# Turning three of attention's five q and k tiles between its units instead of ahead of them

## The chip, the cores and the metric

The kernel runs on one core of a Trainium2 chip. The metric is the device time of one execution in microseconds (us), the median of several runs. The engines named here are TensorE (PE in the profile; its weight loads are PEld), VectorE (DVE), ScalarE (ACT), GpSimd (POOL) and the queue of SyncE (SP), which issues most DMAs. Each engine works through its own list of instructions in the order in which the program wrote them, and waits on semaphores for the others.

## The reference

Three layers follow each other, each on the whole output of the one before: masked attention, and two mixture-of-experts layers. Only the attention is touched.

```python
scores = scale * np.matmul(q, k.transpose(0, 1, 3, 2))       # B, H, S, D = 4, 8, 576, 64
mask_plain = (rel >= 0) & (rel < window)                     # window = 32, heads 0 to 3
mask_dil = (rel >= 0) & (rel < window * dilation) & (rel % dilation == 0)   # dilation = 4, heads 4 to 7
scores = np.where(masks[None, :, :, :], scores, -1000000000.0)
scores = scores - np.max(scores, axis=-1, keepdims=True)
attn = np.exp(scores)
attn = attn / (np.sum(attn, axis=-1, keepdims=True) + 1e-09)
return np.matmul(attn, v).astype(np.float32)
# then x = _moe_ref(attention), result = _moe2_ref(x): routed and balanced experts
```

## The kernel before

`attention` has two parts: it turns q and k into the layout that matmuls need, and then it works through 25 units.

**Turning.** A token's q and k come with the token on the partition; a matmul of scores wants the head dimension there. `TILES` cuts the rows (four tokens in each) into five tiles of 64, 128, 128, 128 and 128 rows. `load_qk` (L103) issues a tile's DMAs on SP. `t_copy` (L149) copies the raw tile with a scale into `rpk` (on DVE) or `rpq` (on ACT). `t_group` (L160) turns four heads with eight transposes on PE (L169) into a PSUM tile; kind 0 is heads 0 to 3, kind 1 heads 4 to 7. `t_evac` (L172) takes that PSUM tile out: ACT writes the fp16 high part (L188), and then DVE subtracts it to get the low part (L190). So a tile has four groups, in the order k kind 0, k kind 1, q kind 0, q kind 1. The evacuation of kind 0 writes with a stride, that of kind 1 in contiguous runs of one or two pieces. The loop at L345 turns all five tiles before the first unit; the loads of a tile go out two tiles ahead, those of v for the units 0 to 2 after the last tile's. Groups take their PSUM tile in turn from `ps_s` (two buffers) and `ps_p` (one), and each is followed by one filler matmul (`warm`, L147).

**Units.** A unit handles 96 queries of four plain heads and 96 of four dilated heads; units 0 and 24 have only one half. In turn n of the loop at L372 the program writes, in this order:

- `scores(n)`: PE, four mask matmuls (L215) and 24 of q with k (L223) into a `ps_s` buffer
- `row_max(n)`: DVE, the maximum over keys (L230) and its scaling (L231)
- `p_trans(n - 1)` on PE (L247, into `ps_p`) and `p_evac(n - 1)`: ACT the high part (L255), DVE the low part (L256)
- `exps(n)`: ACT, eight exponentials from the `ps_s` buffer (L239), which need the row maximum
- `pv(n - 2)`: PE, 24 products with v (L269 to L271) into `ps_v`; DVE the division (L275 to L277)
- `v_split(n + 1)`: DVE the high part of v (L198), POOL two steps (L200, L201)
- `load_v(n + 3)` on SP, and `x_out(n - 3)`: ACT (L288), POOL (L290), stores on SP (L293)

The program is scheduled by hand, so this order is the order on each engine. A PSUM tile is handed out again when the last reader of its buffer is done. What follows attention (the router, then the experts) needs its last output.

Of the kernel before, what the change touches and what calls it, by code (L numbers as in the profile page):

```python
# [11 lines left out]
F32 = mybir.dt.float32  # L12
F16 = mybir.dt.float16
# [6 lines left out]
B, H, S, D = 4, 8, 576, 64  # L20
# [3 lines left out]
QB = 96  # L24
NJ = S // QB
# [37 lines left out]
def tokens_of(p0, n, kind):  # L63


    if kind == 0:
        return [(0, n, p0, 1)]
    out, p = [], p0
    while p < p0 + n:
        r, i = divmod(p, NI)  # L70
        m = min(NI - i, p0 + n - p)
        out.append((p - p0, m, 4 * i + r, 4))
        p += m
    return out
# [9 lines left out]
TILES = [(0, 64), (64, 128), (192, 128), (320, 128), (448, 128)]  # L84
# [4 lines left out]
def attention(tc, q, k, v, masks, wg, ident, xd, L, zero):  # L89

    nc = tc.nc
    with ExitStack() as ctx:
        one = ctx.enter_context(tc.tile_pool(name="a_one", bufs=1))
        ld = ctx.enter_context(tc.tile_pool(name="a_ld", bufs=2))
# [8 lines left out]
        def load_qk(t, nm):  # L103
            f0, n = TILES[t]
            x = raw[t, nm] = ld.tile([128, H, 4, D], F32, name="raw" + nm)
            f = f0
            while f < f0 + n:
                b, i = divmod(f, NI)
                m = min(NI - i, f0 + n - f)
                nc.sync.dma_start(x[f - f0:f - f0 + m].rearrange("i h r d -> i h (r d)"),  # L110
                                  src[nm][b].rearrange("h (i r) d -> i h (r d)", r=4)[i:i + m])
                f += m

        def load_v(u):
            t = VR[u] = vp.tile([128, H, D], F32, name="rawv")
            for kind, (b, j) in UNITS[u].items():
                for p, n, tok, st in tokens_of(max(QB * j - 32, 0), 128, kind):
                    nc.sync.dma_start(t[p:p + n, 4 * kind:4 * kind + 4], bass.AP(
                        tensor=v.tensor, offset=v.offset + (b * H + 4 * kind) * S * D + tok * D,
                        ap=[[st * D, n], [S * D, 4], [1, D]]))  # L120

        def part(u, size):

            ks = list(UNITS[u])
            return slice(ks[0] * size // 2, (ks[-1] + 1) * size // 2)
# [18 lines left out]
        def warm(n):  # L144
            p = ps.tile([128, 2, 512], F32, name="ps_v", bufs=1)
            for _ in range(n):
                nc.tensor.matmul(p[:, 0, :], zero[:, :128], zero, start=True, stop=True)  # L147

        def t_copy(t, nm, eng):  # L149
            n = TILES[t][1]  # L150
            x = RP[t, nm] = ld.tile([128, 4, H, D], F32, name="rp" + nm)
            o, i = x[:n], raw.pop((t, nm))[:n].rearrange("i h r d -> i r h d")
            if eng is nc.scalar:
                nc.scalar.activation(o, i, AF.Copy, scale=SQ)
            else:
                nc.vector.tensor_scalar(o, i, SQ, None, op0=OP.mult)

        GC = [0]

        def t_group(t, nm, kind):  # L160
            f0, n = TILES[t]
            x = RP[t, nm]
            tag, bufs = (("ps_s", 2), ("ps_p", 1), ("ps_s", 2))[GC[0] % 3]
            GC[0] += 1
            p = ps.tile([128, 2, 512], F32, name=tag, bufs=bufs)
            for a in range(2):
                for r in range(4):
                    h = 4 * kind + 2 * a
                    nc.tensor.transpose(p[:, a, r * n:(r + 1) * n], x[:n, r, h:h + 2, :], idf[:n, :n])  # L169
            return p  # L170

        def t_evac(t, nm, kind, p):  # L172
            f0, n = TILES[t]
            pi = p[:, :, :4 * n].rearrange("p a (r i) -> p a r i", r=4)
            if kind == 0:
                parts = [(0, n, [T[nm][:, x, 0:2, 4 * f0:4 * (f0 + n)].rearrange("p a (i r) -> p a r i", r=4)
                                 for x in range(2)])]
            else:
                parts, f = [], f0
                while f < f0 + n:  # L180
                    b, i = divmod(f, NI)
                    m = min(NI - i, f0 + n - f)
                    parts.append((f - f0, m, [
                        T[nm][:, x, 2:4, b * S:(b + 1) * S].rearrange("p a (r i) -> p a r i", r=4)[:, :, :, i:i + m]
                        for x in range(2)]))
                    f += m
            for o, m, (hi, _) in parts:
                nc.scalar.activation(hi, pi[:, :, :, o:o + m], AF.Copy)  # L188
            for o, m, (hi, lo) in parts:
                nc.vector.tensor_sub(lo, pi[:, :, :, o:o + m], hi)  # L190
# [36 lines left out]
        def row_max(u):  # L227
            p, gs = SS[u], part(u, 4)
            nm = wk.tile([QB, 2, 4], F32, name="nm")
            nc.vector.tensor_reduce(nm[:, :, gs], p[:, :, gs], axis=AX.X, op=OP.max)  # L230
            nc.vector.tensor_scalar(nm[:, :, gs], nm[:, :, gs], -SC, None, op0=OP.mult)  # L231
            PP[u] = nm

        def exps(u):
            p, nm, gs = SS.pop(u), PP[u], part(u, 4)
            e = wk.tile([QB, 2, 4, 128], F32, name="e")
            for s in range(2):
                for g in range(gs.start, gs.stop):
                    nc.scalar.activation(e[:, s, g, :], p[:, s, g, :], AF.Exp, bias=nm[:, s, g:g + 1], scale=SC)  # L239
            PP[u] = e  # L240
# [72 lines left out]
        XB, XO = {}, {}  # L313
# [28 lines left out]
        nc.vector.tensor_copy(idh, idf[:QB, :QB])  # L342
        t_copy(0, "k", nc.vector)
        t_copy(0, "q", nc.scalar)
        for t in range(len(TILES)):  # L345
            if t + 2 < len(TILES):
                for nm in "kq":
                    load_qk(t + 2, nm)
            elif t + 2 == len(TILES):
                load_v(0)  # L350
                load_v(1)
                load_v(2)
            for nm in "kq":
                for kind in range(2):
                    t_evac(t, nm, kind, t_group(t, nm, kind))
                    warm(1)
                    if t + 1 < len(TILES) and kind == 0:
                        t_copy(t + 1, nm, nc.vector if nm == "k" else nc.scalar)
            if t == 0:
                nc.scalar.activation(wgh, wgf, AF.Copy, scale=SG)  # L360
                nc.vector.scalar_tensor_tensor(wgl, wgf, SG, wgh, op0=OP.mult, op1=OP.subtract)

        v_split(0)
        loaded = []
        store = [ld.tile([128, 4, H, D], F32, name="rp" + nm).bitcast(F16).rearrange("p r h d -> p (r h d)")
                 for nm in "kkqq"]
        xl = [t[:, :4 * S].rearrange("p (c q) -> p c q", c=4) for t in store[2:]]
        for n in range(NJ + 1):
            XO[(B - 1) * NJ + n] = store[n // 4][:QB, 16 * D * (n % 4):16 * D * (n % 4 + 1)].rearrange(
                "q (k x h d) -> q k x h d", k=2, x=2, h=4)  # L370
        first = S * (B - 1) // 128
        for n in range(NU + 3):  # L372
            if n < NU:
                scores(n)
                row_max(n)
            if 1 <= n <= NU:
                p_evac(n - 1, p_trans(n - 1))
            if n < NU:
                exps(n)
            if n in FILL:  # L380
                warm(FILL[n])
            if n == NU + 1:
                x_turn(NU - 3)
            if 2 <= n <= NU + 1:
                pv(n - 2, [loaded.pop(0)[1] for _ in range(1 if n < NU else 2) if loaded and loaded[0][0] <= n])
            if n + 1 < NU:
                v_split(n + 1)
            if n + 3 < NU:
                load_v(n + 3)
            if n >= 3:  # L390
                x_out(n - 3)
            b, c = divmod(n - 10, NJ)
            if 0 <= b < B - 1 and c < 3:
                c0, c1 = S * b // 128, S * (b + 1) // 128
                c0, c1 = c0 + 2 * c, min(c0 + 2 * c + 2, c1)
                if c1 > c0:
                    x_load(c0, c1)
                    loaded += [(n + 3, i) for i in range(c0, c1)]
            if n == NU - 1:
                x_load(first, first + 1)  # L400
            x_turn(*TURN.get(n, ()))
        p = ps.tile([128, 2, 512], F32, name="ps_v", bufs=1)
# [991 lines left out]
```

## Time and profile before

| what | value |
|---|---|
| median of 3 runs | 1909.49 us (1908.09 to 1910.56) |
| the profiled execution's own time | 1905.73 us |
| its span in the trace | 1904.0 us |
| PE busy, share of the span | 1794.1 us, 94% |
| DVE busy | 1414.7 us, 74% |
| ACT busy | 896.0 us, 47% |
| first exponential of unit 0 | 60.78 us from the span's start |
| first exponential of unit 12 | 106.87 us |
| first exponential of unit 24 | 157.67 us |

The shares are means over stages with different limits. Attention takes the first tenth of the span, so the rows that matter are those of its own stretches. A row of the timeline has its start and its length in us, then engine, line, operation, what it writes and reads, and how many alike are merged; in brackets stands the idle time of the engine before it and what ended it. Instructions overlap a little at their ends on ACT and DVE, so the step from one start to the next is the better measure of what one costs in a row of work.

### The profile page before, as it was taken

To read this page: it belongs to the slowest core of one execution; us is meant where nothing else is said; L and a number is where in the kernel's file an instruction comes from. 1 tells how busy PE (TensorE), PEld (TensorE's weight loads), DVE (VectorE), ACT (ScalarE), POOL (GpSimd) and SP (SyncE) were. 2 spreads that over 40 slices of the span, in tenths; PEclk is the share of its full clock that TensorE was granted. 3 is DMA by queue.
4 is the path that set the end of the run, shared out by engine and by line. 5 is a ranking of instruction groups with operands and counts; after the bars stand their busy time and mean duration, and the time that the engine had idled before them with its cause. 6 is when DMAs were issued, how large, how long until landed. Compare 5 with 4: busy or idle time off the path is not lost.

```text
span 1904.0 us, 36734 instructions
## 1 busy us (share of the span) xinstructions
PE 1794.1 (94%) x15082; PEld 1320.9 (69%) x15082; DVE 1414.7 (74%) x2681; ACT 896.0 (47%) x1558; POOL 284.9 (15%) x359
## 2 busy tenths in 40 slices
PE   6998699989899999999999999999999999999998
PEld 4785366656667665677777777777767777776776
DVE  5996677667764477777788788778878877887666
ACT  6775333333334335554554444455544445554333
POOL 0583321223324000000000000000000000000111
PEclk8888789999999999999999999999999999999999
DMA  9275543355436241233532333353233435323220
GB/s 224 65 153 148 121 96 84 93 99 114 114 68 153 78 152 67 84 150 140 207 126 106 155 150 150 152 195 131 113 144 148 150 148 198 127 115 134 92 92 34
DMA packets 139817, 241.21 MB, mean 127 GB/s; under 512 B 74208, under 2 KB 107232, under 8 KB 132736
## 3 DMA queue, kind: packets, MB, share of 16 engines
q1 hardware_dynamic: 118384, 151.25, 24.4%
q0 software_dynamic: 20592, 87.53, 15.4%
q8 instruction: 118, 1.93, 0.4%
q14 instruction: 51, 0.42, 0.1%
q10 hardware_dynamic: 672, 0.08, 0.0%
HBM read 173.74 MB, written 61.74 MB: 124 GB/s over the span
## 4 chain that ended last, share of the span: by engine, by line
PE 60%; DVE 13%; issue 11%; DMA 8%; ACT 5%; POOL 2%; SPq 1%; POOLq 0%; DVEq 0%; ACTq 0%
PE mm L1058 24%; PE mm L1096 19%; PE mm L800 8%; PE mm L881 4%; DMA raw<-in_w2b_dram 4%; DMA raw<-in_w2a_dram,widx 2%; PE mm L837 2%; DMA rawq<-in_q_dram 1%; DVE nm L230 1%; POOL out_dram L1110 1%; ACT raw L933 1%; DVE hl L1015 1%; PE r L552 1%; DVE w1l L752 1%; POOL xg L781 1%
## 5 line engine op out<-in xcount | busy, mean ns | idle before, releaser
L1058 PE MATMUL mm<-xb,w1h 128*128 128x384 f16 x2352 | 575.8, 327 | 5.1 <-DVE mm L1029 4.7
L1096 PE MATMUL mm<-w2h,hh 128*128 128x256 f16 x1764 | 481.6, 273 | 14.6 <-DVE t L1122 11.8
L1096 PE MATMUL mm<-w2l,hh 128*128 128x256 f16 x1764 | 481.6, 273 | 0.0
L1096 PE MATMUL mm<-w2h,hl 128*128 128x256 f16 x1764 | 481.5, 273 | 0.0
L1096 PEld LDWEIGHTS <-hh 128*128 128x128 f16 x3528 | 345.6, 98 | 59.8 <-issue 17.2
L1058 PE MATMUL mm<-xb,w1l 128*128 128x384 f16 x1176 | 384.8, 327 | 0.0
L1058 PEld LDWEIGHTS <-w1h 128*128 128x128 f16 x2352 | 230.9, 98 | 160.1 <-issue 12.7
L1096 PEld LDWEIGHTS <-hl 128*128 128x128 f16 x1764 | 172.9, 98 | 20.3
L1015 DVE TENSOR_TENSOR hl<-r,hh 128x1536 f16<-128x1536 f32 x84 | 147.5, 1756 | 41.2 <-ACT hh L1014 41.2
L1058 PEld LDWEIGHTS <-w1l 128*128 128x128 f16 x1176 | 115.4, 98 | 76.7 <-issue 1.0
L976 POOL DMA_DIRECT2D ws<-raw x48 | 26.0, 542 | 951.2 <-ACT raw L933 676.1
L1010 ACT ACTIVATE r<-mm 128x384 f32<-128x384 f32 x252 | 119.1, 481 | 98.7 <-PE mm L1058 98.7
L1014 ACT ACTIVATE hh<-r 128x1536 f16<-128x1536 f32 x84 | 124.6, 1483 | 46.0 <-DVE r L1039 44.1
L1021 ACT ACTIVATE mm<-mm 128x384 f32<-128x384 f32 x84 | 40.3, 479 | 179.4 <-PE mm L1058 179.4
L1015 DVE TENSOR_TENSOR hl<-S,hh 128x1152 f16<-128x1152 f32 x84 | 113.5, 1351 | 0.0
L800 PE MATMUL mm<-xt,w1h 128*128 128x288 f16 x512 | 97.8, 290 | 6.3 <-ACT xt L814 6.3
L933 ACT ACTIVATE raw<-raw 128x1024 f16<-128x1024 f32 x48 | 50.6, 1055 | 107.6 <-DVE raw L924 57.6
L803 ACT ACTIVATE w1h<-mm 128x288 f16<-128x288 f32 (+1 forms) x120 | 46.9, 397 | 109.1 <-PE mm L800 105.9
L1106 DVE SCALAR_TENSOR_TENSOR acc<-t,P,acc 128x512 f32<-128x512 f32 x126 | 94.7, 752 | 4.5
L1014 ACT ACTIVATE hh<-S 128x1152 f16<-128x1152 f32 x84 | 96.3, 1147 | 0.0
L800 PE MATMUL mm<-x2l,w0h 128*128 128x256 f16 x288 | 81.9, 284 | 7.4 <-DVE x2l L842 7.4
L804 DVE SCALAR_TENSOR_TENSOR w1l<-mm,w1h 128x288 f16<-128x288 f32 (+1 forms) x120 | 50.8, 435 | 46.7 <-ACT w1h L803 46.3
(288 smaller groups left out, 3307.9 us busy)
## 6 DMA issues: line engine op xcount, KB each, us to landing
xb<-xw SPq DMA_DIRECT2D x30, 1344.0 KB
ws<-raw POOLq DMA_DIRECT2D x48, 448.0 KB, 3.1
ws<-r POOLq DMA_DIRECT2D x48, 448.0 KB, 3.4
raw<-in_w2b_dram SPq DMA_DIRECT2D x32, 512.0 KB
raw<-in_w1b_dram SPq DMA_DIRECT2D x56, 256.0 KB
w1h<-ws SPq DMA_DIRECT2D x6, 1792.0 KB
w1l<-ws SPq DMA_DIRECT2D x6, 1792.0 KB
w2h<-ws SPq DMA_DIRECT2D x6, 1792.0 KB
```

The source lines that it names most:

```text
L800: nc.tensor.matmul(p, a[:, k, 128 * f:128 * (f + 1)], rhs(k, b), start=(k == 0 and i == 0), stop=(k == KT - 1 and i == 2))
L803: nc.scalar.activation(h[0][:, f, :n], p, AF.Relu)
L804: nc.vector.scalar_tensor_tensor(h[1][:, f, :n], p, 0.0, h[0][:, f, :n], op0=OP.max, op1=OP.subtract)
L881: nc.tensor.matmul(p, a[:, f, c], b[:, f, :], start=(f == 0 and n == 0), stop=(f == FT - 1 and n == 2))
L933: self.nc.scalar.activation(hi[:, k], x, AF.Copy, scale=sw)
L1010: nc.scalar.activation(o, p, AF.Relu, scale=SH)
L1014: yield nc.scalar.activation(hq[0][:, i, k], x, AF.Copy)
L1015: yield V.tensor_sub(hq[1][:, i, k], x, hq[0][:, i, k])
L1021: nc.scalar.activation(Q[i], P[i], AF.Copy)
L1058: nc.tensor.matmul(p, w[u][:, 2 * j + i // 2, k, 128 * (i % 2):128 * (i % 2 + 1)], x[:, v, r, j], start=(q in (1, 5) and j == 0 and n == 0 ...
L1096: nc.tensor.matmul(p, h[u][:, i, a, 128 * t:128 * (t + 1)], w[v][:, i, b, :], start=(q in (1, 7) and i == 0 and j == 0), stop=(q in (2, 3) ...
L1106: V.scalar_tensor_tensor(self.acc[:, r, :], x, self.P[:, r, e:e + 1], self.acc[:, r, :], op0=OP.mult, op1=OP.add)
```

## The change

Tiles 0 and 1 are turned ahead of the units as before. The twelve groups of tiles 2, 3 and 4 come from a generator, `later`, of which one step is taken in each of the turns 0 to 11, right behind `exps(n)`: eight transposes, the evacuation on ACT and DVE, and behind a kind 0 group of tiles 2 and 3 the copy of the next tile. Such a group always takes a `ps_s` buffer, the tag of the scores, and has no filler matmul. The loads are written in another order: v for the units 0 and 1 ahead of tile 3, v for unit 2 behind it, tile 4 in turn 0. The tiles that the last units reuse as stores are taken once `later` is done.

```diff
-            tag, bufs = (("ps_s", 2), ("ps_p", 1), ("ps_s", 2))[GC[0] % 3]
+            tag, bufs = (("ps_s", 2), ("ps_p", 1), ("ps_s", 2))[GC[0] % 3] if t < 2 else ("ps_s", 2)
...
-        for t in range(len(TILES)):
-            if t + 2 < len(TILES):
-                for nm in "kq":
-                    load_qk(t + 2, nm)
-            elif t + 2 == len(TILES):
-                load_v(0)
-                load_v(1)
-                load_v(2)
+        def turned(t):
+
             for nm in "kq":
                 for kind in range(2):
                     t_evac(t, nm, kind, t_group(t, nm, kind))
-                    warm(1)
+                    if t < 2:
+                        warm(1)
                     if t + 1 < len(TILES) and kind == 0:
                         t_copy(t + 1, nm, nc.vector if nm == "k" else nc.scalar)
+                    yield
+
+        def later():
+            for t in range(2, len(TILES)):
+                for nm in "kq" if t + 2 < len(TILES) else ():
+                    load_qk(t + 2, nm)
+                yield from turned(t)
+
+        for t in range(2):
+            if t == 1:
+                load_v(0)
+                load_v(1)
+            for nm in "kq":
+                load_qk(t + 2, nm)
+            if t == 1:
+                load_v(2)
+            for _ in turned(t):
+                pass
...
         for n in range(NU + 3):
...
             if n < NU:
                 exps(n)
+            if next(later, 0) == 0 and not store:
+                stores()
             if n in FILL:
                 warm(FILL[n])
```

On DVE, in a full unit of before: `nm` is the row maximum, `ptl` the low part of the turned exponentials, `rc` and `xt` the division, `vh` the high part of v for the next unit, and the last row is the row maximum of the next unit.

```order
L230 TENSOR_REDUCE nm<-ps_s 96x8
L231 TENSOR_SCALAR nm<-nm 96x8
L256 TENSOR_TENSOR ptl<-ps_p,pth 128x768
L275 TENSOR_SCALAR rc<-ps_v 96x8
L276 RECIPROCAL rc<-rc 96x8
L277 TENSOR_TENSOR xt<-ps_v,rc 96x512
L198 TENSOR_SCALAR vh<-rawv 128x8x64
L230 TENSOR_REDUCE nm<-ps_s 96x8
```

The same place now, in turn 4 (tile 3, k, kind 0, and the copy of tile 4's k):

```order
L230 TENSOR_REDUCE nm<-ps_s 96x8
L231 TENSOR_SCALAR nm<-nm 96x8
L256 TENSOR_TENSOR ptl<-ps_p,pth 128x768
L190 TENSOR_TENSOR tk<-ps_s,tk 128x2x4x128
L156 TENSOR_SCALAR rpk<-rawk 128x2048
L275 TENSOR_SCALAR rc<-ps_v 96x8
L276 RECIPROCAL rc<-rc 96x8
L277 TENSOR_TENSOR xt<-ps_v,rc 96x512
L198 TENSOR_SCALAR vh<-rawv 128x8x64
L230 TENSOR_REDUCE nm<-ps_s 96x8
```

The group's subtraction (L190), and the copy (L156) where there is one, stand between a unit's row maximum and the next unit's.

On ACT, two units of before: `e` is the exponentials, `xo` the output's high part, `pth` the turned exponentials' high part.

```order
L239 ACTIVATE e<-ps_s,nm 96x128 x8
L288 ACTIVATE xo<-xt 96x2x256
L255 ACTIVATE pth<-ps_p 128x768
L239 ACTIVATE e<-ps_s,nm 96x128 x8
L288 ACTIVATE xo<-xt 96x2x256
```

The same engine now, in the turns 5 to 7 (the last group of tile 3's k, and tile 3's q):

```order
L188 ACTIVATE tk<-ps_s 128x2x4x16
L288 ACTIVATE xo<-xt 96x2x256
L255 ACTIVATE pth<-ps_p 128x768
L239 ACTIVATE e<-ps_s,nm 96x128 x8
L188 ACTIVATE tq<-ps_s 128x2x4x128
L154 ACTIVATE rpq<-rawq 128x2048
L288 ACTIVATE xo<-xt 96x2x256
L255 ACTIVATE pth<-ps_p 128x768
L239 ACTIVATE e<-ps_s,nm 96x128 x8
```

The group's evacuation (L188) stands right behind a unit's exponentials and ahead of the next unit's.

## Rows read from the trace of the kernel before

**Rows 1.** Windows: us; PE, PEld, DVE, ACT, POOL busy; PEclk; DMA; GB/s.

```profile
0.00:34.00 34.00, 23.64 (x106) 14.99 (x107) 15.74 (x28) 18.70 (x16) 2.26 (x9) 0.75 1.03 221
34.00:59.50 25.50, 17.13 (x129) 12.56 (x129) 23.11 (x18) 21.94 (x18) 0.73 (x1) 0.93 0.44 125
59.50:106.90 47.40, 45.92 (x676) 38.06 (x672) 44.16 (x82) 37.62 (x114) 37.92 (x46) 0.89 0.39 94
```

**Rows 2.** Timeline of DVE in full units (start, length).

```profile
73.67 0.42 DVE L198 TENSOR_SCALAR vh<-rawv 128x512 f16<-128x512 f32 x1
74.00 1.21 DVE L230 TENSOR_REDUCE nm<-ps_s 96x8 f32<-96x1024 f32 x1
...
101.41 1.21 DVE L230 TENSOR_REDUCE nm<-ps_s 96x8 f32<-96x1024 f32 x1
...
103.61 0.15 DVE L275 TENSOR_SCALAR rc<-ps_v 96x8 f32<-96x8 f32 x1
...
104.70 0.75 DVE L198 TENSOR_SCALAR vh<-rawv 128x512 f16<-128x512 f32 x1
105.37 1.21 DVE L230 TENSOR_REDUCE nm<-ps_s 96x8 f32<-96x1024 f32 x1
```

**Rows 3.** Timeline of ACT in the units 0, 11, 12 and 24.

```profile
60.78 1.13 ACT L239 ACTIVATE e<-ps_s,nm 96x128 f32<-96x128 f32 x4 [3.42 <-DVE nm L231]
...
102.92 2.15 ACT L239 ACTIVATE e<-ps_s,nm 96x128 f32<-96x128 f32 x8 [0.60 <-DVE nm L231]
104.94 0.65 ACT L288 ACTIVATE xo<-xt 96x512 f16<-96x512 f32 x1
...
106.87 2.15 ACT L239 ACTIVATE e<-ps_s,nm 96x128 f32<-96x128 f32 x8 [0.59 <-DVE nm L231]
...
157.67 1.13 ACT L239 ACTIVATE e<-ps_s,nm 96x128 f32<-96x128 f32 x4
```

**Rows 4.** Timeline of ACT while the last tile is turned, kinds 0 and 1.

```profile
50.20 2.49 ACT L188 ACTIVATE tk<-ps_p 128x1024 f16<-128x1024 f32 x1 [0.85 <-PE ps_p L169]
52.42 1.13 ACT L188 ACTIVATE tk<-ps_s 128x1024 f16<-128x1024 f32 x1
```

**Rows 5.** Timeline of DVE while tiles are turned.

```profile
32.35 1.33 DVE L190 TENSOR_TENSOR tq<-ps_p,tq 128x640 f16<-128x640 f32 x2
...
45.72 1.23 DVE L156 TENSOR_SCALAR rpk<-rawk 128x2048 f32<-128x2048 f32 x1
46.88 1.26 DVE L190 TENSOR_TENSOR tk<-ps_p,tk 128x896 f16<-128x896 f32 x2
...
52.73 2.42 DVE L190 TENSOR_TENSOR tk<-ps_p,tk 128x1024 f16<-128x1024 f32 x1 [1.10 <-ACT tk L188]
54.96 1.24 DVE L190 TENSOR_TENSOR tk<-ps_s,tk 128x1024 f16<-128x1024 f32 x1
56.13 2.42 DVE L190 TENSOR_TENSOR tq<-ps_s,tq 128x1024 f16<-128x1024 f32 x1
...
59.52 0.27 DVE L198 TENSOR_SCALAR vh<-rawv 128x256 f16<-128x256 f32 x1
```

**Rows 6.** Timeline of PE at its slower pace: a group, parts of units 0 to 2.

```profile
48.20 1.97 PE L169 MATMUL ps_p<-idf,rpk 128*128 128x128 f32 x8 [0.94 <-DVE tk L190]
...
64.61 1.55 PE L247 MATMUL ps_p<-idf,e 96*128 96x96 f32 x8
...
66.19 0.27 PE L269 MATMUL ps_v<-vh,pth 128*96 128x65 f16 x1
...
66.27 0.27 PE L270 MATMUL ps_v<-vh,ptl 128*96 128x65 f16 x1
...
66.91 1.07 PE L215 MATMUL ps_s<-mk,idb 96*96 96x256 bf16 x4
...
67.91 1.51 PE L223 MATMUL ps_s<-tk,tq 64*96 64x128 f16 x24
```

**Rows 7.** Chain that ended last: the transfer behind tile 3's q.

```profile
24.69 13.39 DMA rawq<-in_q_dram
```

More of the change, by code (lines that the diff above doesn't have):

```diff
@@ L364, in attention, with stores @@
         loaded = []
[L365 to L370, printed above, removed]
+        later = later()
+        store, xl = [], []
+        def stores():
+            store.extend(ld.tile([128, 4, H, D], F32, name="rp" + nm).bitcast(F16).rearrange("p r h d -> p (r h d)")
+                         for nm in "kkqq")
+            xl.extend(t[:, :4 * S].rearrange("p (c q) -> p c q", c=4) for t in store[2:])
+            for n in range(NJ + 1):
+                XO[(B - 1) * NJ + n] = store[n // 4][:QB, 16 * D * (n % 4):16 * D * (n % 4 + 1)].rearrange(
+                    "q (k x h d) -> q k x h d", k=2, x=2, h=4)
         first = S * (B - 1) // 128
```

## The prediction

> **What bounds the kernel now.** I read the windows by stage first, then the timelines of DVE, ACT and PE in attention, and last one step of the chain. The windows [rows 1] hold the main fact: DVE is busy 23.11 of 25.50 us while the tiles 2 to 4 are turned, and 44.16 of 47.40 us in the units 0 to 11. Both stretches that the change merges are bound by the same engine. The reader is to see in DVE's timeline [rows 2] that a full unit is one closed row of work: from one row maximum (101.41) to the next (105.37) are 3.96 us without a gap. ACT has room there: its exponentials of unit 12 begin 3.95 us after those of unit 11 (102.92 and 106.87), with 0.59 us of waiting for DVE's row maximum ahead of them [rows 3]. What keeps DVE busy is that ACT and PE work one unit ahead: the scores of unit n+1 go into the second `ps_s` buffer while unit n is still in its exponentials.
>
> **The change part by part.** The work itself stays: twelve groups, their evacuations and the four copies in them cost the same instructions, less twelve filler matmuls on PE, which is not the bound there. New is the order, and it closes a circle between ACT and DVE. In turn n, ACT does the exponentials, then the group's evacuation; DVE's subtraction needs that evacuation; behind the subtraction stand, on DVE, the division of unit n-2, the split of v and the row maximum of unit n+1; and ACT's exponentials of n+1 need that row maximum. Before, nothing on DVE between two row maxima waited for the exponentials of the same turn (the low part `ptl` waits for ACT's L255, which stands ahead of them). So a turn now lasts as long as the circle, each link read from the trace, start to start:
>
> - exponentials to ACT's next instruction: 104.94 - 102.92 = 2.02 us [rows 3]
> - evacuation of kind 0 to the subtraction that waits for it: 52.73 - 50.20 = 2.53 us; of kind 1: 1.13 us and the same 0.04 us of handing over, 1.17 us [rows 4, 5]
> - subtraction to DVE's next instruction: kind 0 54.96 - 52.73 = 2.23 us, kind 1 56.13 - 54.96 = 1.17 us [rows 5]
> - division: 104.70 - 103.61 = 1.09 us; split of v: 74.00 - 73.67 = 0.33 us where POOL is idle, 105.37 - 104.70 = 0.67 us where it is not [rows 2]. I take 0.33, since POOL has a turn twice as long for the same work
> - row maximum to the exponentials: 102.92 - 101.41 = 1.51 us [rows 2, 3]
>
> That is 9.71 us for a turn with a kind 0 group and 7.29 us with kind 1. Six of each make 102.0 us. To this come two copies of k on DVE, in turns 0 and 4: 46.88 - 45.72 = 1.16 us each [rows 5], so 2.3 us. Off go the half-size exponentials of unit 0 (2.15 - 1.13 = 1.0 us [rows 3]) and the division, which the turns 0 and 1 don't have (2.2 us). Together 101.1 us from the exponentials of unit 0 to those of unit 12.
>
> Their start: tile 1's last subtraction ends at 32.35 + 1.33 = 33.68 us [rows 5], and from the split of v for unit 0 to its exponentials are 60.78 - 59.52 = 1.26 us [rows 3, 5]; I add 0.3 us, because PE's scores of unit 0 now wait for that subtraction (half of the 2.51 us from 66.91 to 69.42 [rows 6] is the most that could be). So 35.2 us, and unit 12 begins at 136.3 us against 106.87 us [rows 3]: **29.4 us later**.
>
> What lies beside: the two copies of q on ACT are behind the evacuation, and ACT's next duty, the exponentials, is some 5 us away through DVE, so they cost nothing; in a turn without DVE's part they would cost 1.9 us each (3.8 us). PE has to do, in a turn at its slower pace, the scores (2.51), the turned exponentials (1.55), a group (1.97) and 24 products at 66.27 - 66.19 = 0.08 us (1.92): 7.95 us [rows 6], against 8.5 us for the mean turn. The scores of unit n+1 wait for the exponentials of unit n, since the group holds the other buffer, and end 2.51 us later; DVE comes to their row maximum 1.17 + 1.17 + 1.09 + 0.33 = 3.76 us later at the earliest. So this second new wait is covered, by 1.2 us. If PE were late by more than that, the circle would grow by the excess. The group's transposes are ahead of the exponentials, as they wait only for the subtraction of the turn before.
>
> The moved loads: tile 3's q landed at 24.69 + 13.39 = 38.08 us [rows 7]. Its two MB took 9.5 us at the 221 GB/s of the first window [rows 1], so v for unit 0, now ahead of them, is there by about 30 us (estimate), before DVE asks for it at 33.7. The 0.4 MB of v ahead of tile 3 delay it by 1.8 us; it is wanted by the copies in turns 0 and 2, from 41 us on. Tile 4 and v for unit 3 follow on SP with several turns to spare. If v of unit 0 came behind tile 3 all the same (38.08 + 0.6 us), the start would be 5 us later; I take none. Nothing is queued on SP behind a new wait.
>
> The rest of attention, from unit 12 (106.87) to unit 24 (157.67), is 50.8 us [rows 3] for twelve units that would take 47.5 us at 3.96: 3.3 us of stalls. With the turns stretched these may go (down to -3.3 us), or PE may enter unit 12 at the slower pace and need 5.98 instead of 3.96 us for two units (+4.0 us). I take it as it is. Router and experts need the last output and move with it one to one.
>
> Sum: 1905.73 us of the profiled execution + 29.4 = 1935.1 us. The median lies 3.76 us (0.2%) above that execution, so for a median I forecast 1909.49 + 29.4 = **1938.9 us**. Unknown terms: v's split beside POOL +0.34 in twelve turns (+4.1); the subtraction of a two-piece kind 1 group starting after the first piece, -0.3 in four turns (-1.2); the tail (-3.3 to +4.0). Own range 1934 to 1947.
>
> **The rivals.**
>
> *Not slower, DVE merely full.* If the engines ran ahead far enough that DVE never waits for the evacuation, DVE's own work decides. It idles 2.39 + 3.24 = 5.6 us in the two windows [rows 1], which is the most that merging them can return: 1909.49 - 5.6 = 1903.9 us. The point from which it decides is that the evacuation is done before DVE reaches the subtraction. The order on ACT speaks against it, as the evacuation stands behind the exponentials, which themselves wait for the row maximum in front of the subtraction. The Trainium skill, in "Perfetto Trace Analysis", section "Optimization Strategy", says that where a kernel has regimes with different most-contended engines, interleaving them may help; here the trace shows the same engine in both, so the rule's condition does not hold.
>
> *About the same, only the buffer binds.* If the subtraction hid and only the scores' single buffer counted, the circle were scores, row maximum, exponentials: 2.51 + 1.51 + 2.02 = 6.04 us [rows 2, 3, 6], twelve times 72.5 us, against 106.87 - 35.2 = 71.7 us that the same stretch takes now: 1910.3 us. The same section of the Trainium skill reads a gap that comes back turn after turn on the busy engine as too little PSUM for the next tile. By the rows above such a gap would show ahead of DVE's row maximum, released by PE; I expect it ahead of the subtraction, released by ACT.
>
> *Slower still, PE's clock.* PE works in bursts in a 8.5 us turn. In the first window its granted clock was 0.75, among the units 0.89 [rows 1]. If it stays at 1.2 GHz of its two levels (the other is 2.4), kind 1 turns grow to 7.95 us (+0.66 in six, 4.0 us), and if half of the twelve units behind go at 5.98 us, 12.1 us more: 1938.9 + 16.1 = 1955 us. Against it: a mean of 0.89 over the units says that most of that window ran at the higher level.
>
> **How the numbers follow.** Runs of this kernel tell 0.2% (3.8 us) from no change. The circle gets 0.83, PE's clock 0.09, the buffer alone 0.04, DVE full 0.04. Faster is the last one, 0.04; the same is the buffer alone, 0.04; slower the other two, 0.92. For eight in ten the range is that of the circle, reaching a part of the way to the clock's case and below for terms that I sized too large: 1931 to 1948 us.
>
> **What would show it.** Right: the exponentials (L239) of the units 1 to 12 start 9.7 and 7.3 us apart in turn; DVE idles ahead of every L190 in the units, waiting for ACT's L188, by about 3.7 us for kind 0 (2.02 + 2.53 less what row maximum's tail and `ptl` fill) and 2.4 us for kind 1, some 36 us in all; unit 12 starts near 136 us; from there on everything is 26 to 33 us late. Wrong: no such idle time (DVE full), idle time ahead of L230 released by PE (buffer or clock), a wait for `rawv` or `rawk` early on, or a tail that takes more than 55 us.

## The result

The changed kernel is slower, by the mechanism and nearly by the amount that was forecast. Its median is 1937.78 us (four runs, 1936.44 to 1942.50) against 1910.03 us for the kernel before in the same session (four runs, 1908.09 to 1913.98): 27.75 us between the medians, and a ratio of 1.0127 with a 95% interval of 1.0108 to 1.0147 (the quotient of the two medians, 1.0145, lies in it). The forecast was 1938.9 us.

The first thing to read is ACT's timeline: the row of each unit's exponentials (L239). Columns as in the rows of before: start and length in us, engine, line, operation, what it writes and reads, how many are merged, and in brackets the idle time ahead of it and what ended it.

```profile
36.22 1.13 ACT L239 ACTIVATE e<-ps_s,nm 96x128 f32<-96x128 f32 x4 [3.72 <-DVE nm L231]
44.92 2.14 ACT L239 ACTIVATE e<-ps_s,nm 96x128 f32<-96x128 f32 x8 [4.39 <-DVE nm L231]
...
51.08 0.81 ACT L255 ACTIVATE pth<-ps_p 128x768 f16<-128x768 f32 x1 [3.05 <-PE ps_p L247]
51.78 2.13 ACT L239 ACTIVATE e<-ps_s,nm 96x128 f32<-96x128 f32 x8
...
86.57 2.14 ACT L239 ACTIVATE e<-ps_s,nm 96x128 f32<-96x128 f32 x8 [0.26 <-DVE nm L231]
88.58 2.50 ACT L188 ACTIVATE tq<-ps_s 128x1024 f16<-128x1024 f32 x1
...
96.36 2.14 ACT L239 ACTIVATE e<-ps_s,nm 96x128 f32<-96x128 f32 x8 [2.36 <-DVE nm L231]
...
103.65 2.14 ACT L239 ACTIVATE e<-ps_s,nm 96x128 f32<-96x128 f32 x8 [1.97 <-DVE nm L231]
...
137.49 2.14 ACT L239 ACTIVATE e<-ps_s,nm 96x128 f32<-96x128 f32 x8 [1.85 <-DVE nm L231]
...
186.78 1.12 ACT L239 ACTIVATE e<-ps_s,nm 96x128 f32<-96x128 f32 x4
```

Unit 0 starts at 36.22 us and unit 12 at 137.49, so the twelve turns take 101.27 us; unit 12 is 30.6 us later than in [rows 3], unit 24 29.1 us. The twelve steps between the starts are 8.70, 6.86, 9.43, 7.21, 10.86, 7.29, 9.79, 7.29, 9.75, 7.17, 9.75 and 7.17 us. The two rows at 86.57 and 96.36 are one turn with a kind 0 group, those at 96.36 and 103.65 one with kind 1. In [rows 3] such a step was 3.95 us, with 0.6 us of waiting.

DVE's timeline over the kind 0 turn, which answers to [rows 2, 5]:

```profile
91.11 2.44 DVE L190 TENSOR_TENSOR tq<-ps_s,tq 128x1024 f16<-128x1024 f32 x1 [3.77 <-ACT tq L188]
...
94.52 0.41 DVE L198 TENSOR_SCALAR vh<-rawv 128x512 f16<-128x512 f32 x1
94.85 1.21 DVE L230 TENSOR_REDUCE nm<-ps_s 96x8 f32<-96x1024 f32 x1
...
99.50 1.29 DVE L190 TENSOR_TENSOR tq<-ps_s,tq 128x896 f16<-128x896 f32 x2 [2.38 <-ACT tq L188]
```

The closed row of [rows 2] has a hole in it, always at the same place: ahead of the subtraction (L190), and ACT's evacuation (L188) ends it. The waits of the stretch from 33 to 140 us (us in total, times, longest) add the holes up:

```profile
ACT e L239 <- DVE nm L231: 32.0, 12, 5.3
DVE tk L190 <- ACT tk L188: 18.5, 6, 3.8
DVE tq L190 <- ACT tq L188: 18.1, 6, 3.8
```

DVE waits 36.6 us for ACT, and ACT 32.0 us for DVE: two engines that take turns. The chain that ended last shows it as one path (start, length, what):

```profile
86.57 0.45 ACT e L239 x2
...
88.72 2.37 ACT tq L188
91.11 2.44 DVE tq L190
...
94.52 0.41 DVE vh L198
94.93 1.14 DVE nm L230
96.36 0.33 ACT e L239
```

PE is not in these pieces; in the twelve turns it stands on the chain only in turn 1, for 3.95 us from 47.11 on. The window of the twelve turns, with the columns of [rows 1]:

```profile
34.00:136.00 102.00, 69.04 (x763) 60.52 (x762) 62.72 (x97) 61.00 (x131) 36.57 (x44) 0.74 0.32 79
```

In [rows 1] DVE was 91% and 93% busy in the two stretches that the change merges; now it is busy 62.72 of 102.00 us, 61%, and ACT 60%. No engine is full in the stretch that the change was made for.

The lateness passes to the router unchanged: its first operation on DVE starts at 203.30 us, in the kernel before at 173.57 (+29.7 us). Behind it, the whole times stand as follows; the last column is a traced execution's time over that of before (1905.73 us), less the lateness at the router. The experiments' kernels are those of the next section.

| kernel | lateness at the router, us | whole traced execution, us | added behind it, us |
|---|---|---|---|
| changed | +29.7 | 1942.50 | +7.1 |
| e1_ps_p | +52.4 | 1960.84 | +2.7 |
| e2_no_subtraction | +4.7 | 1905.42 | -5.0 |
| e3_head_of_turn | +23.8 | 1927.73 | -1.8 |
| e4_fillers_back | +29.2 | 1930.74 | -4.2 |
| e5_subtraction_late | +15.9 | 1919.44 | -2.2 |
| e6_before_copies_on_pool | -3.0 | 1901.93 | -0.8 |

The last column varies by 12 us and has no clear trend with the lateness: e4 is as late at the router as the changed kernel and shows -4.2 us where that shows +7.1. So nothing here speaks against experts that move one to one with attention, and the 7.1 us that the changed kernel's traced execution shows behind it (this one was the longest of its four) need not be the change's doing. With a spread of this size behind attention, the ratio's interval (20.6 to 28.1 us of 1910) and the 29.7 us of the traces do not contradict each other; what makes the experts vary was not looked for.

### The profile page after: what moved, and what is told of

Its sections match the earlier page's. It is cut to its first block, busy times and chain, and to the rows that moved or that the text cites. A ratio compares the mean times of both kernels' runs of the same rounds, so it can differ in the third digit from the quotient of the medians.

```text
span 1940.7 us, 36705 instructions
## 1 busy us (share of the span) xinstructions
PE 1798.6 (93%) x15070; PEld 1329.7 (69%) x15070; DVE 1411.7 (73%) x2681; ACT 894.2 (46%) x1558; POOL 287.9 (15%) x359
## 4 chain that ended last, share of the span: by engine, by line
PE 59%; DVE 14%; issue 11%; DMA 8%; ACT 6%; POOL 2%; SPq 0%; POOLq 0%; another core or an unknown queue 0%; DVEq 0%; ACTq 0%
PE mm L1079 24%; PE mm L1117 18%; PE mm L821 8%; DMA raw<-in_w2b_dram 4%; PE mm L902 4%; PE mm L858 1%; ACT e L239 1%; DMA raw<-in_w2a_dram,widx 1%; DVE nm L230 1%; DVE w1l L773 1%; PE r L573 1%; POOL out_dram L1131 1%; DMA rawq<-in_q_dram 1%; ACT raw L954 1%; DVE G L645 1%
```

## The experiments

The theory at the start: the circle ACT exponentials, ACT evacuation, DVE subtraction, DVE row maximum. Its rivals: the `ps_s` buffer that the scores lost to the groups; PE's lower clock in the longer turns; DVE full. Four kernels ran together on one chip (before there: median 1906.76 us of 13 runs), then two on another (before: 1903.46 us of 17). Each kernel is compared with before on its own chip, so the ratios are what to compare.

**The scores' buffer.** In e1 the groups of the tiles 2 to 4 take `ps_p`, and the scores have both `ps_s` buffers again.

```diff
-            ... if t < 2 else ("ps_s", 2)
+            ... if t < 2 else ("ps_p", 1)
```

> As the changed kernel, but the twelve groups between the units take the PSUM tile of the turned exponentials (ps_p, one buffer), so the scores have their two buffers to themselves again. The circle (exponentials, evacuation on ACT, subtraction on DVE, division, split of v, row maximum, exponentials) doesn't go through the scores' buffer: turns stay at 9.7 and 7.2 us, unit 12 begins at 137 us, 1938 us (1934 to 1942). If the scores' lost buffer were the cause, PE's scores would run ahead again, the turns would fall to about 6 us and the time to 1900 to 1915 us.

Measured: 1955.85 us (1952.07 to 1960.84), ratio 1.0249 (1.0208 to 1.0290). The buffer given back returned nothing, but I had not expected that it would cost more. The timeline of ACT and PE in a kind 0 turn and the kind 1 turn behind it:

```profile
93.39 2.15 ACT L239 ACTIVATE e<-ps_s,nm 96x128 f32<-96x128 f32 x8 [0.44 <-DVE nm L231]
...
103.15 2.15 ACT L239 ACTIVATE e<-ps_s,nm 96x128 f32<-96x128 f32 x8 [0.37 <-DVE nm L231]
103.97 1.97 PE L169 MATMUL ps_p<-idf,rpq 128*128 128x128 f32 x8 [2.03 <-DVE ptl L256]
105.98 1.09 ACT L188 ACTIVATE tq<-ps_p 128x896 f16<-128x896 f32 x2 [0.68 <-PE ps_p L169]
...
111.16 0.81 ACT L255 ACTIVATE pth<-ps_p 128x768 f16<-128x768 f32 x1 [3.58 <-PE ps_p L247]
113.60 2.15 ACT L239 ACTIVATE e<-ps_s,nm 96x128 f32<-96x128 f32 x8 [1.64 <-DVE nm L231]
```

This kind 0 turn still takes 9.76 us, and the other five take 8.69 (turn 0), 10.54, 11.64 (with the copy of k), 10.54 and 10.55 us: none is shorter by more than 0.03 us than in the changed kernel, so the circle is there with the scores' buffer free. In the longer ones ACT's evacuation waits for PE's group, 0.68 us in the turn from 113.60, where the group took 1.97 us at a granted clock of 0.51; at 0.85, in the turn shown, a group took 1.09 us and ACT did not wait. The kind 1 turn takes 10.45 us instead of 7.3; the other five take 7.27 to 10.33, and unit 12 starts at 155.34 us. With one `ps_p` buffer for the groups and the turned exponentials, the group waits for the low part `ptl`, which PE's turning of the exponentials feeds, and the next turning waits for the group's subtraction; in this turn 1.9 us more come from DVE's small L231, told below. So the experiment took one buffer circle away and put another in its place. It speaks against the scores' buffer as the cause of the kind 0 turns and tells nothing on the kind 1 turns.

**The subtraction left out.** e2 writes zeros into the low parts of the tiles 2 to 4 at the start (POOL) and does not compute them; its time is therefore not that of the whole computation. In attention its lines are six further down.

```diff
+        for nm in "kq":
...
+                nc.gpsimd.memset(T[nm][:, 1, 2:4, b * S:(b + 1) * S]..., 0.0)
...
-            for o, m, (hi, lo) in parts:
+            for o, m, (hi, lo) in parts if t < 2 else ():
```

> As the changed kernel, but the low parts of the tiles 2 to 4 are set to zero by GpSimd at the start and never computed: the subtraction of the twelve groups is left out, so nothing on DVE between two row maxima waits for ACT's evacuation. Circle: it is cut; the next limit is the scores' single buffer or ACT (exponentials 2.0, evacuation 2.2, two more 1.3 us), 5.0 to 6.9 us a turn, unit 12 begins at 97 to 119 us and the time is 1898 to 1920 us. Only 20 us of DVE work are left out (6 x 2.23 + 6 x 1.17), so more than 20 us saved says that the wait went too. If ACT's added evacuations or PE's clock were the cause and not the wait, unit 12 would begin at 137 less 20 = 117 us or later, and ACT's exponentials would wait for something else than DVE's row maximum.

Measured: 1906.66 us (1904.51 to 1916.37), ratio 1.0012 (0.9989 to 1.0035). Unit 0 starts at 36.84 us and unit 12 at 112.58, 24.9 us earlier than in the changed kernel. Twelve subtractions are 20.4 us of DVE by themselves (six of 2.23 and six of 1.17 us, [rows 5]), so only about 4 us speak for the wait, and the run is a weak witness. It shows better what is next once ACT and DVE are apart. Timeline of ACT and PE in one turn of 6.35 us:

```profile
79.53 2.17 ACT L245 ACTIVATE e<-ps_s,nm 96x128 f32<-96x128 f32 x8
81.75 0.60 PE L221 MATMUL ps_s<-mk,idb 96*96 96x256 bf16 x4 [1.51 <-DVE xt L283]
82.28 1.23 PE L229 MATMUL ps_s<-tk,tq 64*96 64x128 f16 x24
83.44 1.54 PE L253 MATMUL ps_p<-idf,e 96*128 96x96 f32 x8
85.08 0.81 ACT L261 ACTIVATE pth<-ps_p 128x768 f16<-128x768 f32 x1 [1.89 <-PE ps_p L253]
85.88 2.14 ACT L245 ACTIVATE e<-ps_s,nm 96x128 f32<-96x128 f32 x8
```

It is a second circle: exponentials (their last row ends as the scores start), scores, turning of the exponentials, their evacuation on ACT, exponentials. It comes from the buffer, as PE's queue has the scores of n+1, which wait for the exponentials of n, ahead of the turning. In the row at 81.75 the profile names DVE's `xt`, which ends within 0.1 us of the exponentials; in the next turn it names the exponentials (at 88.07, 0.57 us). That next turn, of kind 0, takes 5.48 us, and ACT is busy in all of it: there ACT's own work is the limit.

**The step at the head of the turn.** e3 takes the group's step ahead of `scores(n)` instead of behind `exps(n)`.

```diff
         for n in range(NU + 3):
+            if next(later, 0) == 0 and not store:
+                stores()
             if n < NU:
                 scores(n)
...
                 exps(n)
-            if next(later, 0) == 0 and not store:
-                stores()
```

> As the changed kernel, but the step of the tiles stands at the head of a turn, ahead of the scores, instead of behind the exponentials. The circle keeps exponentials, evacuation, subtraction, row maximum, but the division and the split of v (1.09 + 0.33 us) now stand outside of it, while the output's high part on ACT (0.52 us) comes in: 8.8 and 6.4 us a turn instead of 9.7 and 7.2. Unit 12 begins at 125 us, 12 to 13 us earlier, 1925 us (1921 to 1930). If the circle is not the limit, but the sum of ACT's and DVE's work in a turn, nothing changes: 1938 us.

Measured: 1927.71 us (1924.04 to 1931.35), ratio 1.0108 (1.0066 to 1.0149). The time is near the expected one, with a smaller gain at unit 12, which starts at 130.40: 7.1 us and not 12 to 13. Two things took from it. Unit 0 starts at 39.89 us, 3.7 us later than in the changed kernel, since the first group and a copy of k now stand ahead of its row maximum; and the twelve turns, though 10.8 us shorter (90.51 us), gave less than expected for a reason that the timeline of ACT and PE shows:

```profile
85.60 2.15 ACT L239 ACTIVATE e<-ps_s,nm 96x128 f32<-96x128 f32 x8 [1.39 <-DVE nm L231]
87.80 1.01 PE L215 MATMUL ps_s<-mk,idb 96*96 96x256 bf16 x4 [2.35 <-DVE vh L198]
88.74 1.51 PE L223 MATMUL ps_s<-tk,tq 64*96 64x128 f16 x24
90.18 1.54 PE L247 MATMUL ps_p<-idf,e 96*128 96x96 f32 x8
91.82 0.81 ACT L255 ACTIVATE pth<-ps_p 128x768 f16<-128x768 f32 x1 [2.59 <-PE ps_p L247]
92.53 2.14 ACT L239 ACTIVATE e<-ps_s,nm 96x128 f32<-96x128 f32 x8
...
101.31 2.15 ACT L239 ACTIVATE e<-ps_s,nm 96x128 f32<-96x128 f32 x8 [3.12 <-DVE nm L231]
```

The kind 0 turn takes 8.78 us (101.31 - 92.53), as the first circle with its order changed gives. The kind 1 turn takes 6.93 us: there e2's second circle, with PE at its slower pace, is longer than the first. (The row at 87.80 names DVE's split of v, which ends 0.05 us behind the exponentials; at 94.75 the scores start ahead of that split, so they do not wait for it.)

**The fillers back.** e4 puts one filler matmul behind every group again, as before.

```diff
-                    if t < 2:
-                        warm(1)
+                    warm(1)
```

> As the changed kernel, with the filler matmul behind each of the twelve groups put back. Circle: PE is not in it; turns stay at 9.7 and 7.2 us and the time at 1938 us (1934 to 1942), whatever the granted clock between 34 and 136 us (0.74 without the fillers). If PE's lower clock there costs time, the clock rises with the fillers and the time falls by several us.

Measured: 1931.57 us (1930.72 to 1933.33), ratio 1.0131 (1.0093 to 1.0169), the same as the changed kernel's. The turns are the same to some hundredths (86.60, 96.39 and 103.69 are the starts that were 86.57, 96.36 and 103.65), and unit 12 starts at 137.57. Its window beside that of the changed kernel:

```profile
34.00:136.00 102.00, 76.35 (x768) 61.99 (x767) 62.69 (x96) 60.11 (x130) 36.60 (x44) 0.70 0.32 80
```

PE is 7.3 us busier and no turn changed. The granted clock did not rise, so the run does not show what a higher one would give back. The changed kernel's own trace does: its kind 0 turn from 86.57 took 9.79 us at a granted clock of 0.85, the one from 103.65 took 9.75 at 0.68. For these turns PE's clock is out as a cause; turn 1, with PE on the chain, ran at 0.50.

**The subtraction later.** e5 is the test that keeps all work. It splits a group's step: transposes and evacuation behind `pv`, the subtraction (and a copy of k) one turn later on DVE, behind the next unit's row maximum. In attention its lines are up to five further down.

```diff
                 row_max(n)
+            if due:
+                due[0]()
+                if due[1]:
+                    t_copy(due[1], "k", nc.vector)
             if 1 <= n <= NU:
                 p_evac(n - 1, p_trans(n - 1))
             if n < NU:
                 exps(n)
-            if next(later, 0) == 0 and not store:
-                stores()
...
                 pv(n - 2, ...)
+            due = next(later, None)
```

> As the changed kernel, with all its work, but the subtraction of a turn's group (and the copy of k behind it) stands on DVE behind the next unit's row maximum, and the group itself behind the products with v. Circle: it is cut without leaving anything out, since the exponentials of unit n+1 no longer wait for a subtraction that waits for ACT's evacuation in turn n. DVE's idle time ahead of the twelve subtractions (36.6 us in the changed kernel) goes nearly to nothing. Left are the two PSUM buffers: subtraction, next group, next scores, in PE's order, 6.2 us a turn at PE's faster pace and 8.1 us at its slower one, so unit 12 begins at 109 to 135 us instead of 137.5 and the time is 1908 to 1934 us, most likely near 1920. If the order on DVE were not the cause, the turns stay at 9.7 and 7.2 us and the time at 1935 to 1938 us.

Measured: 1918.70 us (1917.39 to 1922.99), ratio 1.0080 (1.0057 to 1.0103). Unit 0 starts at 36.95 us, unit 12 at 123.11: 14.4 us earlier than in the changed kernel. DVE's timeline in one turn, then the waits of the stretch:

```profile
82.38 1.22 DVE L235 TENSOR_REDUCE nm<-ps_s 96x8 f32<-96x1024 f32 x1 [1.76 <-PE ps_s L228]
...
83.72 2.43 DVE L192 TENSOR_TENSOR tq<-ps_s,tq 128x1024 f16<-128x1024 f32 x1
```

```profile
DVE nm L235 <- PE ps_s L228: 18.1, 11, 2.4
...
PE ps_s L169 <- DVE tk L192: 14.1, 6, 3.9
...
PE ps_s L169 <- DVE tq L192: 7.8, 4, 3.0
```

The subtraction (L192 here) starts right behind the row maximum, and none of the twelve waits for ACT, where the changed kernel lost 36.6 us. So the circle is shown: the same work in an order that opens it gives back nearly half of the loss at unit 12 (14.4 of 30.6 us). The group also moved behind `pv` on PE, but PE was on the changed kernel's chain in turn 1 alone, so by the chain that move can't be what gave most of the time back. What is left is the buffer: DVE waits for PE's scores, and PE's group for the subtraction that empties its buffer. It is shorter than the first circle, 86.16 us for twelve turns against 101.27, and so it was hidden behind it.

**Relief for the tiles in the kernel before.** Where DVE is full, a copy can go to an engine that is not. e6 is the kernel before with the copies of k for the tiles 2 to 4 on POOL.

```diff
-                nc.vector.tensor_scalar(o, i, SQ, None, op0=OP.mult)
+                eng.tensor_scalar(o, i, SQ, None, op0=OP.mult)
...
-                        t_copy(t + 1, nm, nc.vector if nm == "k" else nc.scalar)
+                        t_copy(t + 1, nm, (nc.vector if t == 0 else nc.gpsimd) if nm == "k" else nc.scalar)
```

> The kernel before, with the copies of k of the tiles 2 to 4 on GpSimd instead of DVE. If DVE is what bounds the turning of the tiles (23.1 of 25.5 us busy), two copies of 1.16 us leave its row of work and unit 0 and all behind begin 2 to 3 us earlier (first exponential near 58 us instead of 60.8); in the time 2 us, 0.1%, hardly to be told from no change. If GpSimd takes over 8 us for a copy, the next tile's k waits for it and unit 0 begins later.

Measured: 1901.82 us (12 runs, 1899.48 to 1905.99), ratio 0.9988 (0.9978 to 0.9999). Its median is 1.6 us below that of the kernel before, 0.1%, at the edge of what the runs can tell. The timeline of POOL, DVE and ACT:

```profile
33.46 5.38 POOL L156 TENSOR_SCALAR rpk<-rawk 128x2048 f32<-128x2048 f32 x1 [2.63 <-PE ps_s L169]
...
43.43 2.43 DVE L190 TENSOR_TENSOR tk<-ps_s,tk 128x1024 f16<-128x1024 f32 x1 [1.18 <-ACT tk L188]
...
59.82 1.13 ACT L239 ACTIVATE e<-ps_s,nm 96x128 f32<-96x128 f32 x4 [3.42 <-DVE nm L231]
```

Unit 0 starts 0.96 us earlier than in [rows 3], not the 2 to 3 us expected, and less than one of the copies had taken from DVE (1.16 us, [rows 5]): DVE now waits longer for ACT's evacuations (1.18 us in the row shown, 0.53 ahead of the same subtraction before, at 43.46), and ACT was nearly as busy all along (21.94 of 25.50 us in [rows 1]). Unit 12 starts at 104.83 us, 2.0 us earlier.

## Why the prediction was right

**The circle.** The six terms of the sum came out of rows of before, and the turns of after repeat them: kind 0 was worked out as 9.71 us and took 9.75 to 9.79 in three of the four turns that have neither a copy of k nor a missing division (9.43 in turn 2, where unit 0's division is of half size, 0.79 us for 1.09: the sum had it full); kind 1 as 7.29 against 7.17 to 7.29. The copy of k was to add 1.16 us to turn 4, and it took 10.86 us (9.71 + 1.16 = 10.87). The whole stretch was forecast as 101.1 us and took 101.27; that it is so close is in part luck, as turn 1 was 0.66 us longer than its sum and turn 2 0.28 shorter. The -1.2 us for two-piece groups did not come: their turns 3, 5 and 7 took 7.21 to 7.29 us, the one-piece turns 9 and 11 7.17. The idle time ahead of L190 was forecast as some 36 us, 3.7 and 2.4 us each, and is 36.6, with 3.77 and 2.38 in the two turns shown. The split of v beside POOL, for which 4.1 us stood in the range, took 0.33 us to DVE's next instruction in the turn shown (94.52 to 94.85), the value taken.

**The second new wait** was said to be covered by 1.2 us. It was, as no row maximum waited for PE in the twelve turns. But turn 1, without a division, should have taken 7.29 - 1.09 = 6.20 us and took 6.86, and there ACT waited 3.05 us for PE's turned exponentials (L255 at 51.08). I had closed that circle through the row maximum (2.51 + 1.51 + 2.02 = 6.04 us in the second rival). e2 and e3 show that it closes through the turning on PE and its evacuation on ACT, with 6.35 and 6.93 us. Twelve such turns are 76.2 to 83.2 us and not 72.5, so the second rival, "about the same", was worked out some 4 to 11 us too low and belonged on the slower side. That it did not decide saved the forecast from this; it is what e3 and e5 then ran into.

**The start.** Unit 0 was to begin at 35.2 us and began at 36.22. The missing 1.0 us is in one small instruction; timeline of DVE and POOL of the changed kernel:

```profile
34.12 0.69 DVE L230 TENSOR_REDUCE nm<-ps_s 96x4 f32<-96x512 f32 x1
34.83 1.28 POOL L200 TENSOR_TENSOR vsc<-rawv,c 128x512 f32<-128x512 f32 x1
34.84 1.29 DVE L231 TENSOR_SCALAR nm<-nm 96x4 f32<-96x4 f32 x1
```

In the kernel before the same L231 took 0.26 us (at 60.42), as POOL's product (60.59) began behind it. Here it begins 0.01 us behind POOL's and ends with it.

**The loads.** v for unit 0 was estimated at about 30 us; POOL's first use of it starts at 29.86, ended by `rawv`. Tile 3 was to be there by 39.9 us (38.08 + 1.8, [rows 7]), ahead of its first copy at 41 us. That copy, of its k, started at 41.95 us with no idle time of DVE ahead of it: the step from the subtraction before, 39.72 to 41.95 us, is the 2.23 us of [rows 5]. The chain has a row `32.78 9.17 DMA rawk<-in_k_dram` just ahead of this copy, which reads as a transfer that landed at the last moment. SP's timeline tells otherwise:

```profile
26.59 2.74 SPq L110 DMA_DIRECT2D rawk<-in_k_dram  x2
...
32.78 2.81 SPq L110 DMA_DIRECT2D rawk<-in_k_dram  x1
```

Tile 3's k went out in two DMAs at 26.59; the one at 32.78 is tile 4's, which a later copy uses (75.18). So the chain's row does not show when tile 3's k landed, nor how much cover it had. The 38.08 us that the prediction took from [rows 7] is such a reading too: in the kernel before that row ends as the copy of q starts, behind work of ACT, so it is the latest that the tile can have landed. No copy waited in the turns, so the loads cost nothing there; the size of their delay is not shown.

**The tail** was taken as it is, with -3.3 to +4.0 us as bounds: from unit 12 to unit 24 it took 49.3 us (186.78 - 137.49) against 50.8, 1.5 us less. With the start 1.0 us late and the turns 0.2 us longer, that nearly balances: +29.1 us at unit 24 where +29.4 was forecast.

**The rivals.** DVE is not full (61%), so the rival in which its own work decides is out. The Trainium skill's rule, in "Perfetto Trace Analysis", section "Optimization Strategy", that a gap which comes back on the busy engine can mean too little PSUM, was weighed in the prediction: the gap came, ended by ACT and not by PE, and e1, which gave the scores their second buffer back, was slower. Behind the circle, in e5 and in turns of e2 and e3, the buffer is what binds, as that rule has it. PE's granted clock was 0.74 in the stretch, between its two levels, and the rival's price for it did not come: kind 1 turns took 7.17 to 7.29 us and not 7.95, and the tail got shorter. Only turn 1, 0.66 us over its sum, had PE on the chain at the slower pace.

## What to carry to other kernels

Before moving work into a loop of engines that run their queues in order, follow the moved piece's inputs and outputs through the queues: if it starts behind an instruction of the loop on one engine and stands ahead of that instruction's own input on another, the engines take turns, and the turn's length is the sum of the links, whatever room each engine had. The sum can be worked out beforehand from the start-to-start steps of a trace in which the two pieces are still apart. When a circle is opened, the next longer one takes over: look for it, and close it through every engine whose queue it passes, not through the shortest path.

## What the runs showed of the hardware

- A DVE instruction on 96 x 4 elements took 1.29 us instead of 0.26 beside a product on POOL, and in e1 one on 96 x 8 took 2.05 us instead of 0.17 (at 111.46) while POOL went through a subtraction and a product (111.07 to 113.48), and ended within 0.03 us of the product. The Trainium skill, in "SBUF — State Buffer", section "Who interferes with whom", says that DVE and GpSimd share a pair of ports as an exclusive lock, and that where DVE's instruction runs in one of its two-port modes, which a `tensor_scalar` can enter, the one that issues first blocks the other for its whole instruction. The trace agrees in the first case: POOL's row began 0.01 us earlier, and both end within 0.02 us. No row shows DVE's mode, and in e1 POOL's product began behind DVE's instruction (112.22 and 111.46), which the rule alone does not explain.
- A scaled copy of 128 x 2048 f32 takes 1.23 us on DVE, 1.99 us on ACT (L154, at 90.79 in the changed kernel) and 5.38 us on POOL.
- The granted clock of TensorE from 34 to 136 us was 0.74, 0.70 and 0.62 (changed kernel, e4, e1), against 0.93 and 0.89 in [rows 1]. In e5, with shorter turns, it was 0.82 in the same window. The changed kernel's kind 0 turns did not differ with it (9.79 us at 0.85, 9.75 at 0.68); e1's, in which ACT waits for PE's group, did (9.76 us at 0.85, 10.54 at 0.51).
